# A fourth buffer for the words of the first 40 halves, in the tile of the slot sums and choices, and four halves fetched ahead

## The chip, the cores and the metric

The kernel runs on one core of one Trainium2 chip. The time is that of the device in microseconds (us); lower is better. A core has a matrix engine (TensorE, "PE"; "PEld" is its weight load), a vector engine (VectorE, "DVE"), an activation engine (ScalarE, "ACT"), a general engine (GpSimd, "POOL") and a fifth one (SyncE, "SP") that here does nothing but issue transfers. Each engine takes its own instructions strictly in the order in which they were written for it, and waits at an instruction whose inputs aren't there.

## What is computed

Three parts follow one another. Attention with a decay, over 4 x 8 heads of 576 tokens and 64 columns, gives `x` (2304 tokens by 512). A gated unit multiplies two products of `x`. A soft mixture of experts reduces 2304 tokens to 32 slots, runs 8 experts on the slots and spreads the result over the tokens again.

```python
scores = scale * np.matmul(q, k.transpose(0, 1, 3, 2))
cum = np.cumsum(np.maximum(s, 0.0), axis=-1)
scores = np.where(causal, -1e9, scores + np.minimum(-(cum[..., :, None] - cum[..., None, :]), 0.0))
attn = softmax(scores);  x = np.matmul(attn, v)          # then (2304, 512)
...
a = x @ w1;  b = x @ w2
h = a * b @ w3;  x = h @ w_out                           # w1, w2, w3, w_out are float64
...
logits = x @ phi
d = softmax(logits, over tokens);  slot_input = d.T @ x  # 32 slots
slot_out[e] = np.maximum(slot_input[e] @ w1[e], 0.0) @ w2[e]
c = softmax(logits, over slots);  out = c @ slot_out
```

The four weights of the gated unit come as float64, and the kernel has to turn their 64-bit words into float32 by itself.

## The kernel before

**Words and halves.** The float64 weights lie in HBM as 64-bit integers ("words"). They come in tiles of 128 by 1024 words, and each tile in two halves of 128 by 512 words, 512 KB each. The list `TODO` gives the order: 8 tiles of `w12` (w1 and w2 together), 4 of `wot` and 8 of `w3t` (w_out and w3 turned), which are the first 40 halves, k = 0 to 39 (`N0` = 20 tiles); then 4 of `wo` and 8 of `w3`, which are loaded later in another way. For each half:

- `fetch_words(k)` issues one transfer on SP (L178) into a tile of the tag "words", of which there are `NRAW` = 3. A transfer into a buffer has to wait until the half that lay in it has been converted.
- `convert` makes float32 of it: one pass on ACT (L192), then three on DVE (L195, L196, L199), or for `wot` and `w3t` a second pass on ACT (L203) and two on DVE (L204, L207). In the rows the words are `raw_w`, `raw_wot` and `raw_w3t`.
- For `w12` the result is split in two parts, on ACT (L223) and POOL (L224), for the matrix products of the gated unit.
- `load(k)` does one step of this: it converts half k, and behind that it fetches half k + 3.

**Attention.** `att_fetch` loads q and k of one item (L287, L288, L290, into a tile also named `raw`), `att_prep` the rows of the decay (L312, L314), and `att_values` v (L298). The decay rows are worked out at the start and stored to HBM by `decay_store` (L166, L167, into `rows_d`); from the third item on they are read back from there. `att_scores` makes the scores (PE L349, DVE L352, ACT L357), `att_norm` scales them (L366, L367 on DVE, L370 on POOL), `att_transpose` turns them (PE L385, L399; ACT L387, L401), `att_pv` multiplies by v (`x_ps`, L110).

**Gated unit and slots.** `glu_half` is a group of 12 products (`gl`, L447). `slot_sums` adds into `z_acc` (128 by 512 floats), `slot_choice` writes `c_all` (128 by 20 by 32 floats).

**Order.** All steps of a stage are written as short functions and interleaved by their weights (`weave`). Three stages carry the first 40 halves: k = 0 to 7 beside the first attention items, k = 8 to 25 beside the second group of items and the first 16 groups of the gated unit, the rest beside the third group. A scheduler may then reorder the instructions of PE, DVE, ACT and POOL within what their data allow, by its own estimate of when each can run. SP alone keeps the order as written.

The four lines on which the change turns are these:

```python
raw = ap.tile([P, 512], I64, tag="words", name=f"raw_{kind}_{i}_{e}", bufs=NRAW)
nc.sync.dma_start(raw, ...)
...
if k + NRAW < 2 * N0:
    fetch_words(k + NRAW, ap)
```

Of the kernel before, what the change touches and what calls it, by code (L numbers as in the profile page):

```python
# [10 lines left out]
F32 = mybir.dt.float32  # L11
# [3 lines left out]
I64 = mybir.dt.int64  # L15
# [6 lines left out]
P = 128  # L22
# [6 lines left out]
NS = NE * SPE  # L29
# [18 lines left out]
def attn_glu_softmoe_kernel(  # L48
# [17 lines left out]
    cp = pool("const", 1)  # L66
# [17 lines left out]
    NW, NRAW, NG4, NX, NE_ = 8, 3, 4, 6, 11  # L84
# [34 lines left out]
    ident = cp.tile([P, P], F32, name="ident")  # L119
    v_sb = cp.tile([P, FC, NS], F32, name="v_sb")  # L120
    v_last = cp.tile([P, ND, 4, NS], F32, name="v_last")
    z_acc = cp.tile([P, 512], F32, name="z_acc")
    run_max = cp.tile([P, 2], F32, name="run_max")
    run_sum = cp.tile([P, 2], F32, name="run_sum")
    c_all = cp.tile([P, 20, NS], F32, name="c_all")

    rsum_t = [cp.tile([P, 5, 2], F32, name=f"rsum_{k}") for k in range(3)]
    for t in rsum_t:
# [41 lines left out]
    words = {}  # L170
    TODO = [("w12", i) for i in range(FC)] + [("wot", i) for i in range(4)] + [("w3t", i) for i in range(FC)]
    N0 = len(TODO)
    TODO += [("wo", i) for i in range(4)] + [("w3", i) for i in range(FC)]

    def fetch_words(k, ap):
        (kind, i), e = TODO[k // 2], k % 2
        raw = ap.tile([P, 512], I64, tag="words", name=f"raw_{kind}_{i}_{e}", bufs=NRAW)
        nc.sync.dma_start(raw, {"w12": w12, "wo": wo, "w3": w3, "wot": wot, "w3t": w3t}[kind][i, :, 512 * e : 512 * e + 512])  # L178
        words[k] = raw

# [94 lines left out]
    def att_fetch(n, ap):  # L275
        h, tiles = ITEMS[n]
        if h % 2 == 0:
            b, c = divmod(h // 2, H // 2)
            for blk, (_, nt, own) in enumerate(BLK):
                if own[0] in tiles:  # L280
                    x_t[b, blk, c] = xpl.tile([P, 2, nt], F32R, tag=f"x{blk}", name=f"x_{b}_{blk}_{c}", bufs=NX)
        q0, q1 = QT[tiles[0]][0], sum(QT[tiles[-1]])
        tag = ("raw", "qa", "qb")[n % 3] if n < NF32 else "raw"
        raw = ap.tile([P, 2, S], F32, tag=tag, name=f"raw_{n}", bufs=NRW)
        m = 64 if n < NF32 else P
        if q0:
            nc.sync.dma_start(raw[:m, 0, q0:q1], qk[h, 0, :m, q0:q1])  # L287
            nc.sync.dma_start(raw[:m, 1, :q1], qk[h, 1, :m, :q1])  # L288
        else:
            nc.sync.dma_start(raw[:m, :, :q1], qk[h, :, :m, :q1].rearrange("n p t -> p n t"))  # L290
        hd[n] = dict(raw=raw, q0=q0, q1=q1)
# [455 lines left out]
    with tc.tile_pool(name="att", bufs=1) as ap:  # L747
        phi_sb = ap.tile([P, KC, NS], F32, name="phi_sb")
        u_sb = ap.tile([P, FC, NS], F32, name="u_sb")
        decay_fetch()  # L750
        fetch_words(0, ap)
        att_fetch(0, ap)
        fetch_words(1, ap)
        att_fetch(1, ap)
        make_identity(nc, ident)
# [10 lines left out]
        for n in range(NDIR):  # L766
            att_prep(n, ap)
        att_fetch(2, ap)
        for k in range(2, NRAW):
            fetch_words(k, ap)  # L770
        decay_store()
        for n in range(NDIR, FAR):
# [14 lines left out]
        def load(k):  # L787
            i = k // 2 - 1
            if FC <= i < N0:
                (sum_rows if k % 2 else use_rows)(*TODO[i])  # L790
            if k < 2 * N0:
                load_words(k, ap)
            if k + NRAW < 2 * N0:
                fetch_words(k + NRAW, ap)

        def fetch_later(i):
            if i > N0:
                store_words(i - 1)
            if i < len(TODO):
                for e in range(2):  # L800
                    fetch_words(2 * i + e, ap)

        prep = [(1, lambda k=k: load(k)) for k in range(2 * N0 + 2)]
        more = []
        for i in range(N0, len(TODO)):
# [10 lines left out]
        k = GC - GB  # L816
# [12 lines left out]
    def big(where, name):  # L829
        if where == "w":  # L830
            return wp.tile([P, 2048], F32, tag="W", name=name, bufs=NW)
        if where == "t":
            return tp2.tile([P, 2048], F32, name=name)
        return ep.tile([P, 2048], F32, tag="E", name=name)
# [3 lines left out]
    for i in range(2):  # L838
        t = big("e", f"wo_t{i}").rearrange("p (i c) -> p i c", i=2)
# [3 lines left out]
    for i in range(4):  # L843
        t = big("e", f"w3_t{i}").rearrange("p (i c) -> p i c", i=2)
# [67 lines left out]
    for q in range(4):  # L912
        cols = slice(256 * q, 256 * q + 256)
        yps = psum(("acc", "sg")[q % 2], f"y_ps_{q}")
        for r in range(2):
            for j in range(4):
                f = 4 * r + j
# [10 lines left out]
    for r in range(2):  # L928
        for c in range(2):
            for j in range(4):  # L930
                f = 4 * r + j
# [199 lines left out]
```

## Time and profile before

| | us |
|---|---|
| median of 3 runs | 554.52 |
| the three runs | 548.87, 554.52, 554.88 |
| the profiled execution | 550.8 |
| its span, from first to last instruction | 549.0 |
| PE busy in it | 516.8 (94%) |
| DVE, ACT, POOL busy | 328.9, 310.7, 130.7 |

The profiled execution is one of its own, beside the three runs. 1.8 us of it lie outside the span. "Busy" of PE means that a product was under way, which isn't the same as PE at its peak: products overlap, and their ends are modelled.

### The profile page before, as it was taken

Reading aid. Unit: us, or ns where it says so; the run is one execution under the profiler, and the core shown is the slowest. Engines: PE = TensorE matmul, PEld = TensorE weight load, DVE = VectorE, ACT = ScalarE, POOL = GpSimd, SP = SyncE. Lnnn points to the kernel's source line nnn. Section 1 sums busy time; section 2 is a strip of 40 time slices with the busy share of each in tenths; the row PEclk is TensorE's granted clock in tenths of the full one; section 3 lists DMA queues with packets and bytes.
Section 4 is the critical chain, followed back from the end, with each engine's and each line's share of the span. In section 5 each row is a group of like instructions: output and inputs, shape, how many; then the busy total and the mean of one; then the engine's idle time right before and its main releaser. Section 6 shows DMA issues by size and latency. Waiting matters only on the chain.

```text
span 549.0 us, 11760 instructions
## 1 busy us (share of the span) xinstructions
PE 516.8 (94%) x4288; PEld 433.6 (79%) x4288; DVE 328.9 (60%) x1014; ACT 310.7 (57%) x845; POOL 130.7 (24%) x199
## 2 busy tenths in 40 slices
PE   2898899999899999999999999999999999989993
PEld 2577688787788898989979899899989899843452
DVE  7568797879886484866667668467631211252433
ACT  4576676778785574766677567558644211321222
POOL 5475663103553241111211311111310000000000
PEclk9999999999899999999999999999999999999998
DMA  5856965877673263563557437453504999689977
GB/s 145 251 160 192 282 219 194 282 242 254 206 230 112 88 170 109 164 204 127 170 171 221 165 104 225 155 172 125 162 39 152 414 412 365 245 293 424 421 294 240
DMA packets 38809, 118.03 MB, mean 215 GB/s; under 512 B 4224, under 2 KB 10560, under 8 KB 35296
## 3 DMA queue, kind: packets, MB, share of 16 engines
q1 hardware_dynamic: 36768, 113.60, 61.0%
q10 hardware_dynamic: 1984, 3.69, 2.4%
q8 instruction: 34, 0.56, 0.4%
q14 instruction: 23, 0.19, 0.1%
HBM read 102.11 MB, written 11.60 MB: 207 GB/s over the span
## 4 chain that ended last, share of the span: by engine, by line
PE 70%; DMA 12%; DVE 9%; issue 3%; ACT 2%; POOL 1%; SPq 1%; DVEq 0%; ACTq 0%; POOLq 0%
PE gl L447 31%; PE x_ps L110 7%; PE sc_ps L349 7%; DMA raw_w<-in_w 5%; PE pt_ps L385 5%; PE gn_ps L617 3%; PE o_ps L1032 3%; PE h_ps L994 3%; DMA raw_w3t<-in_w3t 3%; PE ptd_ps L399 2%; PE z_ps L110 2%; DMA raw<-in_qk 2%; DVE sc L352 1%; PE lg L110 1%; POOL sc L370 1%
## 5 line engine op out<-in xcount | busy, mean ns | idle before, releaser
L447 PE MATMUL gl<-x,w12t 128*128 128x320 f32 (+1 forms) x1536 | 236.2, 303 | 1.0 <-DVE gC L465 1.0
L447 PEld LDWEIGHTS gl<-x,w12t 128*128 128x128 f32 x1536 | 211.2, 189 | 8.9 <-issue 4.2
L370 POOL TENSOR_SCALAR sc<-sc,rinv 128x64 f32<-128x64 f32 (+4 forms) x160 | 100.8, 648 | 254.1 <-DVE rinv L367 77.4
L357 ACT ACTIVATE sc<-sc,nmax 128x64 f32<-128x64 f32 (+4 forms) x160 | 89.9, 564 | 30.7 <-DVE nmax L352 28.2
L352 DVE CUSTOM_DVE_ANT_0 sc<-sc_ps,mask 128x64 f32<-128x64 f32 (+4 forms) x160 | 65.0, 422 | 32.4 <-PE sc_ps L349 31.5
L387 ACT COPY pt<-pt_ps 128x128 f32<-128x128 f32 (+3 forms) x128 | 52.8, 425 | 34.9 <-PE pt_ps L385 26.0
L385 PE MATMUL pt_ps<-ident,sc 128*128 128x128 f32 x320 | 56.9, 287 | 4.7 <-POOL sc L370 2.3
L385 PEld LDWEIGHTS pt_ps<-ident,sc 128*128 128x128 f32 x320 | 38.6, 145 | 16.5 <-issue 7.1
L453 ACT COPY a<-gl 128x256 f32<-128x256 f32 (+1 forms) x64 | 25.4, 399 | 45.5 <-PE gl L447 40.3
L349 PE MATMUL sc_ps<-qa 128*128 128x64 f32 (+1 forms) x144 | 46.8, 337 | 2.0 <-DVE gT L465 0.8
L110 PE MATMUL x_ps<-pt,v 128*64 128x256 f32 (+1 forms) x384 | 47.4, 358 | 0.0
L349 PE MATMUL sc_ps<-raw 68*128 68x288 f32 (+4 forms) x96 | 35.3, 513 | 11.1 <-DMA raw<-rows 9.6
L349 PE MATMUL sc_ps<-qb 68*128 68x64 f32 (+1 forms) x144 | 43.9, 307 | 0.1
L110 PEld LDWEIGHTS x_ps<-pt,v 128*64 128x64 f32 x384 | 33.5, 140 | 5.8 <-issue 1.0
L349 PEld LDWEIGHTS sc_ps<-raw 68*128 68x128 f32 x96 | 21.1, 260 | 16.1 <-issue 12.2
L192 ACT ACTIVATE w_w<-raw_w 128x512 f32<-128x512 f32 x32 | 21.5, 673 | 18.4 <-DMA raw_w<-in_w 18.3
L435 DVE TENSOR_TENSOR x<-x_ps,x 128x320 fp32r<-128x320 f32 (+1 forms) x32 | 14.1, 452 | 29.1 <-ACT x L434 29.1
L620 ACT COPY gn<-gn_ps 128x512 f32<-128x512 f32 x40 | 22.6, 586 | 15.5 <-PE gn_ps L617 14.9
L349 PEld LDWEIGHTS sc_ps<-qa 128*128 128x128 f32 x144 | 27.7, 193 | 4.3 <-DVE gT L465 1.3
L357 ACT ACTIVATION_READ_ACCUMULATOR sc<-sc,nmax 128x1 f32 x160 | 31.0, 194 | 0.0
L349 PEld LDWEIGHTS sc_ps<-qb 68*128 68x128 f32 x144 | 27.7, 192 | 0.9 <-issue 0.5
L399 PE MATMUL ptd_ps<-ident,sc 128*128 128x128 f32 x160 | 26.4, 291 | 2.1 <-ACT pt L387 1.9
(180 smaller groups left out, 726.5 us busy)
## 6 DMA issues: line engine op xcount, KB each, us to landing
ew<-in_ew SPq DMA_DIRECT2D x27, 1024.0 KB
raw_w<-in_w SPq DMA_DIRECT2D x32, 512.0 KB
raw<-in_qk SPq DMA_DIRECT2D x24, 576.0 KB
v<-in_v SPq DMA_DIRECT2D x16, 576.0 KB
raw_w3t<-in_w3t SPq DMA_DIRECT2D x16, 512.0 KB
raw_wot<-in_wot SPq DMA_DIRECT2D x8, 512.0 KB
raw_wo<-in_wo SPq DMA_DIRECT2D x8, 512.0 KB
w_d<-w_w SPq DMA_DIRECT2D x8, 512.0 KB
```

The costliest lines, as they stand in the source:

```text
L110: mm = nc.tensor.matmul(out_, lhs, rhs, start=start, stop=stop)
L192: line_up(nc.scalar.activation(out=w, in_=hi.bitcast(F32), func=AF.Copy, scale=F64_SCALE))
L349: nc.tensor.matmul(pp[:r, : z - a], x[:, 0, q0 : q0 + r], x[:, 1, a:z], start=x is mul[0], stop=x is mul[-1])
L352: nc.vector.tensor_tensor_reduce(out=sc[:r, a:z], in0=pp[:r, : z - a], in1=hd["mask"][:r, m0 : m0 + z - a], scale=-0.125, scalar=3.0e38 if ...
L357: nc.scalar.activation(out=sc[:r, :W], in_=sc[:r, :W], func=AF.Exp, bias=nmax[:r, i : i + 1], scale=-1.0, accum_out=rsum[:r, i, 0:1],)
L370: nc.gpsimd.tensor_scalar(out=sc, in0=sc, scalar1=rinv[:, i : i + 1], scalar2=1.0, op0=ALU.mult, op1=ALU.mult)
L385: nc.tensor.transpose(tp[:, j * P : (j + 1) * P], sc[:, j * P : (j + 1) * P], ident)
L387: t["turned", i] = nc.scalar.copy(out=pt[:, p0 : p0 + step * (i - 1) + 1 : step], in_=tp[:, : i * P].rearrange("p (j q) -> p j q", q=P))
L399: nc.tensor.transpose(dg[:, p0 : p0 + P], t["sc"][:, c0 : c0 + P], ident)
L447: nc.tensor.matmul(acc[:, :nt], w12_t[fc][:, wi, n, kc], x_t[b, blk, kc][:, xi], start=k == 0, stop=k == 3 * KC - 1)
L453: st["a_copy"] = nc.scalar.copy(out=a_sb[:, :nt], in_=acc[:, :nt])
L620: st["turned", blk, k, h] = nc.scalar.copy(out=gn[:r, 4 * h : 4 * h + 4].rearrange("p c f -> p (c f)"), in_=tp[:r])
```

## The change

The tiles `z_acc` and `c_all` become two parts of one tile, `spare_words`, of the same total size (4608 bytes in each partition). Nothing is written to either of them until the first 40 halves have been converted, in the order of the program. Up to then 4096 bytes of it serve as a fourth buffer: of the first 40 halves, every fourth (k = 3, 7, ... 39) goes there, the other three of four go to the tiles of the tag "words". Before the loop four halves are fetched instead of three, and `load(k)` fetches half k + 4 instead of k + 3. Only the first 40 halves are concerned. Line numbers behind the change are higher by one to four: L178 becomes L182, L192 becomes L196, L357 becomes L361, L166 becomes L167, and so on.

```diff
-    z_acc = cp.tile([P, 512], F32, name="z_acc")
+    spare_words = cp.tile([P, 256 + 10 * NS], I64, name="spare_words")
+    z_acc = spare_words.bitcast(F32)[:, :512]
...
-    c_all = cp.tile([P, 20, NS], F32, name="c_all")
+    c_all = spare_words.bitcast(F32)[:, 512:].rearrange("p (t s) -> p t s", s=NS)
...
     def fetch_words(k, ap):
         (kind, i), e = TODO[k // 2], k % 2
-        raw = ap.tile([P, 512], I64, tag="words", name=f"raw_{kind}_{i}_{e}", bufs=NRAW)
+        if k < 2 * N0 and k % (NRAW + 1) == NRAW:
+            raw = spare_words[:, :512]
+        else:
+            raw = ap.tile([P, 512], I64, tag="words", name=f"raw_{kind}_{i}_{e}", bufs=NRAW)
...
         att_fetch(2, ap)
-        for k in range(2, NRAW):
+        for k in range(2, NRAW + 1):
             fetch_words(k, ap)
         decay_store()
...
-            if k + NRAW < 2 * N0:
-                fetch_words(k + NRAW, ap)
+            if k + NRAW + 1 < 2 * N0:
+                fetch_words(k + NRAW + 1, ap)
```

On SP, at the start of the program, this stood in a row before (`raw_w_1_0` is half 2, `raw_w_1_1` half 3; `rows_d` are the decay rows, `raw_156`, `raw_163` and `raw_180` are q and k of the third to fifth attention item):

```order
L290 DMA raw_156<-in_qk 64x2x320
L178 DMA raw_w_1_0_158<-in_w 128x512
L166 DMA rows_d<-rows_130 32x4x512
L166 DMA rows_d<-rows_131 32x4x512
L167 DMA rows_d<-rows_132 256x1x64
L290 DMA raw_163<-in_qk 64x2x320
L314 DMA raw_156<-rows_d 4x2x320
L298 DMA v_176<-in_v 128x640
L314 DMA raw_163<-rows_d 4x2x320
L290 DMA raw_180<-in_qk 64x2x320
L178 DMA raw_w_1_1_209<-in_w 128x512
```

And now (`spare_words` is half 3, `raw_w_2_0` half 4):

```order
L294 DMA raw_155<-in_qk 64x2x320
L182 DMA raw_w_1_0_157<-in_w 128x512
L182 DMA spare_words<-in_w 128x512
L167 DMA rows_d<-rows_129 32x4x512
L167 DMA rows_d<-rows_130 32x4x512
L168 DMA rows_d<-rows_131 256x1x64
L294 DMA raw_163<-in_qk 64x2x320
L318 DMA raw_155<-rows_d 4x2x320
L302 DMA v_176<-in_v 128x640
L318 DMA raw_163<-rows_d 4x2x320
L294 DMA raw_180<-in_qk 64x2x320
L182 DMA raw_w_2_0_209<-in_w 128x512
```

The fetch of half 3 moved up past the stores of the decay rows, and half 4 stands where half 3 stood. So it goes on: at each later place of a fetch on SP the next half is fetched.

On ACT, a little later at the start, the conversion of half 3 stood behind the first softmax passes (L357) of the third item before:

```order
L192 ACTIVATE w_w_1_0_317<-raw_w_1_0_158 128x512
L357 ACTIVATE sc_167,rsum_94<-sc_167,nmax_186 128x192
L357 ACTIVATE sc_167,rsum_94<-sc_167,nmax_186 128x320
L387 COPY pt_218<-pt_ps_1_220 128x128
L387 COPY pt_218<-pt_ps_2_223 128x2x128
L223 CAST w12t_316<-w_w_1_0_317 128x512
L401 COPY ptd_219<-ptd_ps_227 128x192
L357 ACTIVATE sc_233,rsum_95<-sc_233,nmax_232 128x64
L357 ACTIVATE sc_233,rsum_95<-sc_233,nmax_232 128x192
L192 ACTIVATE w_w_1_1_381<-raw_w_1_1_209 128x512
```

And now:

```order
L196 ACTIVATE w_w_1_0_317<-raw_w_1_0_157 128x512
L361 ACTIVATE sc_167,rsum_93<-sc_167,nmax_186 128x192
L196 ACTIVATE w_w_1_1_381<-spare_words 128x512
L361 ACTIVATE sc_167,rsum_93<-sc_167,nmax_186 128x320
L391 COPY pt_218<-pt_ps_1_220 128x128
L391 COPY pt_218<-pt_ps_2_223 128x2x128
L227 CAST w12t_316<-w_w_1_0_317 128x512
L405 COPY ptd_219<-ptd_ps_227 128x192
```

The conversion of half 3 moved up by seven places, ahead of a softmax pass of the second item. Elsewhere on ACT, DVE, POOL and PE instructions changed places by up to 39 rows; the last sixth of the list of PE and the last twelfth of those of ACT and DVE stand as they stood.

## Rows read from the trace of the kernel before

**Rows 1.** Busy time by stretch: us, busy us of each engine, clock, DMA share, GB/s.
```profile
14.00:41.00 27.00, 23.97 (x89) 17.64 (x90) 15.39 (x65) 18.12 (x62) 14.99 (x25) 1.00 0.68 204
41.00:82.00 41.00, 37.02 (x253) 29.71 (x250) 35.13 (x78) 28.67 (x72) 23.93 (x21) 1.00 0.77 232
55.00:69.00 14.00, 11.77 (x83) 9.26 (x82) 10.97 (x23) 8.73 (x22) 8.58 (x8) 1.00 0.96 284
82.00:123.00 41.00, 39.58 (x304) 32.27 (x302) 32.67 (x84) 30.05 (x72) 6.50 (x8) 1.00 0.71 240
123.00:165.00 42.00, 39.17 (x361) 33.45 (x360) 37.91 (x116) 34.36 (x99) 19.58 (x24) 0.96 0.69 226
206.00:274.00 68.00, 68.00 (x579) 63.03 (x579) 42.91 (x133) 42.43 (x117) 13.18 (x25) 1.00 0.50 156
274.00:412.00 138.00, 137.21 (x1173) 125.79 (x1172) 88.79 (x281) 89.56 (x251) 28.84 (x51) 1.00 0.49 153
```

**Rows 2.** Chain that ended last, pieces that are transfers: start us, us, what.
```profile
11.61 4.83 DMA rows_d<-rows
...
23.27 4.93 DMA raw_w<-in_w
...
44.47 4.82 DMA raw_w<-in_w
...
54.64 7.27 DMA raw_w<-in_w
...
109.50 5.68 DMA raw_w3t<-in_w3t
...
122.42 4.33 DMA raw_w3t<-in_w3t
...
153.40 4.56 DMA raw_w3t<-in_w3t
```

**Rows 3.** Timeline of ACT, conversions behind these transfers; in brackets the idle before.
```profile
28.28 0.67 ACT L192 ACTIVATE w_w<-raw_w 128x512 f32<-128x512 f32 x1 [0.89 <-DMA raw_w<-in_w]
...
49.37 0.66 ACT L192 ACTIVATE w_w<-raw_w 128x512 f32<-128x512 f32 x1 [0.89 <-DMA raw_w<-in_w]
...
61.99 0.67 ACT L192 ACTIVATE w_w<-raw_w 128x512 f32<-128x512 f32 x1 [0.63 <-DMA raw_w<-in_w]
...
115.21 0.68 ACT L192 ACTIVATE w3t<-raw_w3t 128x512 f32<-128x512 f32 x1 [0.95 <-DMA raw_w3t<-in_w3t]
...
126.77 0.67 ACT L192 ACTIVATE w3t<-raw_w3t 128x512 f32<-128x512 f32 x1 [1.15 <-DMA raw_w3t<-in_w3t]
...
157.98 0.71 ACT L192 ACTIVATE w3t<-raw_w3t 128x512 f32<-128x512 f32 x1 [1.21 <-DMA raw_w3t<-in_w3t]
```

**Rows 4.** Waits of ACT from 14 to 165 us: total us, times, longest.
```profile
ACT w_w L192 <- DMA raw_w<-in_w: 9.6, 8, 2.2
ACT w3t L192 <- DMA raw_w3t<-in_w3t: 7.5, 8, 1.4
...
ACT wot L192 <- DMA raw_wot<-in_wot: 2.4, 2, 2.2
```

**Rows 5.** Timeline of ACT, conversion of half 2.
```profile
15.14 0.67 ACT L192 ACTIVATE w_w<-raw_w 128x512 f32<-128x512 f32 x1 [1.47 <-DMA raw_w<-in_w]
```

**Rows 6.** Timeline of SP: start us, us, what it issues.
```profile
10.45 0.59 SPq L178 DMA_DIRECT2D raw_w<-in_w  x1
11.15 0.84 SPq L166 DMA_DIRECT2D rows_d<-rows  x2
...
19.14 0.59 SPq L178 DMA_DIRECT2D raw_w<-in_w  x1
...
53.51 0.52 SPq L178 DMA_DIRECT2D raw_w<-in_w  x1
```

**Rows 7.** Waits of SP's queue from 14 to 165 us: total us, times, longest.
```profile
SPq L178 <- DVE w3t L207: 38.4, 12, 5.6
...
SPq L178 <- DVE wot L207: 10.7, 5, 3.8
```

**Rows 8.** Instructions on `raw_w3t`, and on `c_all`: duration ns, first and last start us.
```profile
L178 SPq DMA_DIRECT2D raw_w3t<-in_w3t x16: 327/328/329, 101.3 to 156.5; - x16
...
L207 DVE SCALAR_TENSOR_TENSOR w3t<-raw_w3t,w3t x16: 651/678/1059, 109.4 to 168.3; 128x512 int32<-128x512 int32 x16
...
L542 DVE TENSOR_TENSOR c_all<-ct_ps,mx x12: 177/216/226, 195.2 to 485.3; 128x64 f32<-128x64 f32 x8, 64x32 f32<-64x32 f32 x4
```

## The prediction

> **What bounds the kernel now.** I read the busy time by stretch first. From 206 to 412 us PE is the bound and nothing else can be: it is busy 68.00 of 68 us and then 137.21 of 138, with DVE and ACT at under two thirds [rows 1]. All 40 halves have been converted by then: the last DVE pass on them starts at 168.3 us [rows 8]. So the change can't speed anything up behind some 170 us. What it can do is bring the point at which PE becomes full forward or push it back, and the rest, which is a fixed amount of PE work, moves with that point. The first 165 us are another regime. There PE does 89 products in the 27 us from 14 to 41 and 253 in the next 41, against 579 in 68 later [rows 1]: it is called busy most of the time, but it waits inside that. DVE is the fullest of the others, 35.13 of 41 us, 32.67 of 41 and 37.91 of 42 [rows 1].
>
> Then the chain of waits, to see what ends last in those 165 us. Transfers of words stand in it six times behind the first one [rows 2], so words do come late. How late is on the timeline of ACT, which is the first to touch a half: it stands idle before these six conversions for 0.89, 0.89, 0.63, 0.95, 1.15 and 1.21 us [rows 3], 5.7 us together. A transfer on the chain lasts 4 to 7 us, but only this last bit of it is time in which ACT had nothing else. Over the whole stretch from 14 to 165 us ACT waited 9.6 + 7.5 + 2.4 = 19.5 us for words [rows 4]; 1.47 of it were for half 2 [rows 5], whose fetch the change leaves where it is. 18.0 us are within reach of it.
>
> **The change part by part.** *Earlier fetches.* Each half from k = 3 on is fetched at the place where the half before it was fetched. For half 4 that is the place of 19.14 us instead of 23.27 [rows 2, 6], 4.1 us earlier; for the one fetched at 54.64 us it is the place of 53.51, 1.1 us earlier [rows 2, 6]. Against that stand lags of 0.63 to 1.21 us, so each of the six should be gone, the one at 61.99 us by the smallest margin, since it falls into the stretch where the DMA engines are 0.96 busy [rows 1, 3]. The gain is between 0 (ACT takes up the lag at once, but DVE is late next) and 18.0 us (every wait of ACT comes through to PE). I take the 5.7 us of the six waits on the chain, and count the other 12.3 at nothing, because DVE, busy 106 of the 124 us from 41 to 165 [rows 1], or the loads of v and of q and k come last there.
>
> *The start.* The fourth fetch stands ahead of the stores of the decay rows. On SP it takes 0.59 us to issue [rows 6]; that is the least that the stores come later. At the most they also come later by the 512 KB that go ahead: at the 284 GB/s of the fullest stretch [rows 1] that is 1.85 us, 2.4 together. The stores are on the chain: they took 4.83 us [rows 2], although their own 576 KB would take 2.1 at that rate; half 2 was issued just ahead of them at 10.45 us [rows 6], and 1.85 + 2.1 is most of the 4.83. That speaks for the upper end. Against it, from 14 to 41 us the DMA engines are only 0.68 busy [rows 1], so that the queue empties again and half 3 is missing from it later, at 19.14 us. I take the middle, 1.5 us.
>
> The Trainium skill has a rule on this ("DMA: Bandwidth & Descriptors", section "Queues, rings and completion order"): on each DMA engine descriptors of one queue are consumed in the order of its ring. By that rule the whole 512 KB stand ahead of the stores, and the loss would be 2.4 us and the net gain 3.3 instead of 4.2. The 4.83 us of the stores agree with it; no row shows what part of it reaches the end.
>
> *The order on the other engines.* The conversion of half 3 now stands ahead of a softmax pass of the second item on ACT. Half 2 was ready at 15.14 us [rows 5]; half 3 comes behind it by 1.85 us, at 17.0, so ACT waits there and then works 0.67 us. That delays copies which PE needs only for the first product with v, and the third item's scores wait for the decay rows anyway, so I put it at nothing while the stores are the later of the two; without that cover it costs some 1.5 us. The many small moves behind it I put at nothing too: where PE is full they can cost it no more than the 0.8 us by which it isn't full from 274 to 412 [rows 1]; before that they may go either way, and the range has to hold that.
>
> *What costs nothing.* The tile is no larger than the two it replaces. A fetch into the fourth buffer waits for the conversion of the half four back, at the place on SP where a fetch waited for the same conversion before: SP waits there as it did (38.4 and 10.7 us for `w3t` and `wot` [rows 7]), and v and the q and k behind it come neither sooner nor later for it, unless the conversions themselves come sooner. The first write of `c_all` is at 195.2 us, 27 us behind the last pass on the words [rows 8]; that distance covers the new dependence between them.
>
> Sum: 5.7 - 1.5 = 4.2 us off. The profiled execution of 550.8 us would become 546.6. It lies 3.7 below the median of the three runs; against that median, 554.5, the forecast is 550.3.
>
> **The rivals.** *The ring of buffers sets the pace.* The sixteen fetches of `w3t` are issued from 101.3 to 156.5 us [rows 8], one every 3.68 us, and twelve times SP waited for a conversion there [rows 7]. If the round trip (fetch, land, convert, fetch again) is what holds this stretch, three halves go through it in 11.0 us; four would do so in the same time, 2.76 us each, 13.8 us less over the 15 steps. DVE allows at most its idle time from 82 to 165 us, 83 - 70.6 = 12.4 [rows 1]. With the loss at the start that is 10.9 us off, 543.6. For it: the eight waits of ACT for `w3t` [rows 4]. Against it: each of them is at most 1.4 us of a period of 3.68, so most of the period is other work.
>
> *Something else is late by as much.* ACT's waits vanish, and DVE or the loads of v, q and k end at the same moment as before. Then only the start is left: 0 to 2.4 us more, near 555. For it: DVE is at 85% from 41 to 165 us. Against it: DVE itself is not full.
>
> *The words overtake attention.* At the start the stores lose 2.4 us and the early conversion 1.5 on ACT, and nothing is won: 3.9 us more, 558.4. This decides the sign as soon as the words' lag gives back less than 3.9 us, which is two thirds of what I count on. For it: attention, not the words, feeds PE at the start, and the stores were on the chain [rows 2]. Against it: the words fetched ahead are the same bytes, only sooner, and the queue has room.
>
> **How the numbers follow.** One per cent, about what a measurement of this kernel can tell from no change, is 5.5 us: 549.0 to 560.1. Chances: the forecast 0.42 (547 to 553); the pace of the ring 0.25 (539.5 to 547); something else late 0.17 (553 to 557); overtaken 0.16 (556 to 562). Faster by over 1%: all but a little of the second and a third of the first, 0.38. Slower by over 1%: the upper half of the last, 0.09. The rest, 0.53, is within 1%. The range of 541.5 to 557 leaves out the best third of the second case and most of the last, together about 0.2; it takes in both ends of the start's price.
>
> **What the profile after would show.** Waits of ACT for words from 14 to 165 us fall from 19.5 to a few us, and no transfer of words stands in the chain between 20 and 165 us. The last pass on `w3t` starts some 4 us sooner than 168.3, and everything behind it is shifted by that and otherwise alike. The stores of the decay rows land near 18 us instead of 16.4. Under the pace of the ring the fetches of `w3t` would come every 2.8 us; under the third case ACT's waits would have gone and the last pass still start near 168. I would be wrong if the words' lag were only the shadow of another wait, or if the order on PE, which moved in the whole first part, turned out better or worse by more than the words are worth.

## The result and the profile after

The changed kernel is slower: 559.94 us in the median of four runs (557.26 to 561.31) against 551.85 for the kernel before on the same chip (548.87 to 554.88, four runs). The ratio is 1.0138, interval 1.0096 to 1.018. The forecast was 550.3. The profiled execution took 560.15 us, its span 558.4. Medians and ratios in this document leave out the slow executions: one of 1703 us, one of 1255 us, and three of the kernel before between 554.8 and 557.4 us. In the lines of the changed kernel, L438 is the copy that takes the sums of v (L110) out of PSUM, before it was L434.

Busy time by stretch, columns as in [rows 1]:

```profile
14.00:41.00 27.00, 19.24 (x73) 13.71 (x73) 16.18 (x58) 16.10 (x51) 14.36 (x23) 1.00 0.66 187
41.00:82.00 41.00, 37.61 (x192) 28.25 (x192) 26.62 (x73) 25.63 (x67) 17.90 (x20) 0.75 0.69 204
82.00:123.00 41.00, 41.00 (x281) 32.71 (x281) 31.67 (x79) 29.56 (x69) 10.59 (x12) 1.00 0.67 223
...
274.00:412.00 138.00, 137.66 (x1196) 126.17 (x1198) 93.13 (x296) 91.98 (x254) 34.32 (x55) 1.00 0.51 160
```

Look at the counts beside PE and at the clock, not at the busy time. From 41 to 82 us PE is called busy for as long as before (37.61 against 37.02), but it does 192 products instead of 253, and the granted clock is 0.75 instead of 1.00 [rows 1]. DVE does 26.62 us of work there instead of 35.13. By the table further down the seventh fetch of v goes out 12.8 us late, the twelfth 9.4, and the span ends 9.4 us late (558.4 against 549.0). So the loss was made in the first 85 us, where the forecast expected three of the six waits to go.

The pieces of the chain of waits that are transfers of words, start and us:

```profile
11.05 6.13 DMA spare_words<-in_w
...
25.39 6.03 DMA raw_w<-in_w
...
117.95 7.13 DMA spare_words<-in_w3t
...
128.25 5.44 DMA spare_words<-in_w3t
134.72 6.39 DMA raw_w3t<-in_w3t
...
155.91 4.42 DMA spare_words<-in_w3t
```

Words are fetched earlier, and still they stand in the chain [rows 2]. The waits of ACT from 14 to 165 us say how that can be:

```profile
ACT w_w L196 <- DMA raw_w<-in_w: 8.2, 5, 2.1
...
ACT wot L196 <- DMA raw_wot<-in_wot: 4.3, 5, 1.3
...
ACT spare_words L207 <- DMA spare_words<-in_w3t: 2.9, 1, 2.9
...
ACT w_w L196 <- DMA spare_words<-in_w: 2.6, 2, 2.1
```

With the smaller rows of this view (1.8, 1.6, 0.8 and 0.3) they sum to 22.5 us, against 19.5 before [rows 4]. The conversions have moved forward in ACT's order along with the fetches, and wait as they did. A new wait is on SP, same stretch:

```profile
SPq L302 <- PE x_ps L110: 54.8, 8, 10.6
SPq L182 <- DVE w3t L211: 21.7, 11, 3.2
```

and in the kernel before:

```profile
SPq L298 <- PE x_ps L110: 19.4, 5, 6.8
```

SP's queue now stands 54.8 us for the sums of v (it may not load a v before PE is done with an older one), and everything that is written behind it, q, k, decay rows and words, stands with it. When these fetches of v are issued is a good clock for the whole first part. The times are those of SP's timeline; the runs in the lower rows come further down:

| kernel | 1st fetch of v | 3rd | 4th | 5th | 7th | 9th | 12th |
|---|---|---|---|---|---|---|---|
| before | 17.26 | 32.73 | 42.49 | 51.53 | 71.58 | 104.36 | 171.47 |
| after | 19.37 | 36.64 | 50.24 | 60.70 | 84.41 | 116.53 | 180.86 |
| after, order of before | 20.43 | 35.70 | 44.02 | 52.32 | 70.85 | 103.57 | 168.86 |
| before and idle load, order of before | 20.07 | 36.39 | 46.07 | 56.16 | 76.30 | 109.54 | 176.76 |
| own order from 41 us on | 20.13 | 35.66 | 49.59 | 64.11 | 84.18 | 120.09 | 183.84 |
| own order up to 41 us | 20.39 | 38.78 | 48.29 | 56.60 | 75.60 | 108.31 | 171.69 |

After is 2.1 us late at the first, 3.9 at the third, 7.8 at the fourth and 12.8 at the seventh.

### The profile page after: what moved, and what is told of

It reads as the page before. It is cut to its first block, busy times and chain, and to the rows that moved or that the text cites. A ratio compares the mean times of both kernels' runs of the same rounds, so it can differ in the third digit from the quotient of the medians.

```text
span 558.4 us, 11762 instructions
## 1 busy us (share of the span) xinstructions
PE 522.2 (94%) x4288; PEld 435.9 (78%) x4288; DVE 326.1 (58%) x1014; ACT 313.1 (56%) x845; POOL 127.9 (23%) x199
## 4 chain that ended last, share of the span: by engine, by line
PE 75%; DMA 9%; ACT 8%; DVE 4%; issue 2%; SPq 1%; ACTq 0%; DVEq 0%
PE gl L451 32%; PE sc_ps L353 9%; PE x_ps L110 8%; PE pt_ps L389 6%; PE gn_ps L621 3%; DMA spare_words<-in_w3t 3%; PE o_ps L1036 3%; PE h_ps L998 3%; PE ptd_ps L403 3%; ACT sc L361 2%; PE z_ps L110 2%; DMA raw_w<-in_w 2%; DMA raw_wo<-in_wo 1%; PE lg L110 1%; DMA raw_w3t<-in_w3t 1%
## 5 line engine op out<-in xcount | busy, mean ns | idle before, releaser
L451 PE MATMUL gl<-x,w12t 128*128 128x320 f32 (+1 forms) x1536 | 240.3, 306 | 2.2 <-DVE gC L469 1.5
L451 PEld LDWEIGHTS gl<-x,w12t 128*128 128x128 f32 x1536 | 214.7, 192 | 10.3 <-issue 4.6
L374 POOL TENSOR_SCALAR sc<-sc,rinv 128x64 f32<-128x64 f32 (+4 forms) x160 | 97.4, 627 | 257.1 <-DVE rinv L371 108.0
L361 ACT ACTIVATE sc<-sc,nmax 128x64 f32<-128x64 f32 (+4 forms) x160 | 89.9, 563 | 29.0 <-DVE nmax L356 27.7
L356 DVE CUSTOM_DVE_ANT_0 sc<-sc_ps,mask 128x64 f32<-128x64 f32 (+4 forms) x160 | 65.5, 423 | 38.4 <-PE sc_ps L353 34.9
L353 PE MATMUL sc_ps<-raw 68*128 68x288 f32 (+4 forms) x96 | 37.8, 537 | 12.9 <-DMA raw<-rows 9.6
L110 PE MATMUL x_ps<-pt,v 128*64 128x256 f32 (+1 forms) x384 | 47.8, 361 | 0.0
L110 PEld LDWEIGHTS x_ps<-pt,v 128*64 128x64 f32 x384 | 32.6, 142 | 7.5 <-issue 2.6
L361 ACT ACTIVATION_READ_ACCUMULATOR sc<-sc,nmax 128x1 f32 x160 | 30.8, 192 | 0.0
L469 DVE TENSOR_TENSOR gU<-gl,a 128x256 f32<-128x256 f32 (+1 forms) x20 | 8.7, 435 | 34.4 <-PE gl L451 28.1
L228 POOL TENSOR_TENSOR w12t<-w_w,w12t 128x512 fp32r<-128x512 f32 x16 | 23.2, 1456 | 20.8 <-ACT w12t L227 20.7
```

Source lines behind the costliest of these rows:

```text
L110: mm = nc.tensor.matmul(out_, lhs, rhs, start=start, stop=stop)
L228: nc.gpsimd.tensor_tensor(out=tl, in0=w, in1=th.bitcast(F32), op=ALU.subtract)
L353: nc.tensor.matmul(pp[:r, : z - a], x[:, 0, q0 : q0 + r], x[:, 1, a:z], start=x is mul[0], stop=x is mul[-1])
L356: nc.vector.tensor_tensor_reduce(out=sc[:r, a:z], in0=pp[:r, : z - a], in1=hd["mask"][:r, m0 : m0 + z - a], scale=-0.125, scalar=3.0e38 if ...
L361: nc.scalar.activation(out=sc[:r, :W], in_=sc[:r, :W], func=AF.Exp, bias=nmax[:r, i : i + 1], scale=-1.0, accum_out=rsum[:r, i, 0:1],)
L374: nc.gpsimd.tensor_scalar(out=sc, in0=sc, scalar1=rinv[:, i : i + 1], scalar2=1.0, op0=ALU.mult, op1=ALU.mult)
```

## The experiments

Each kernel was timed in five rounds beside the kernel before on the same chip. Medians of before were 551.2, 550.5, 549.8, 551.5 and 549.0 us for the five groups below, so runs of different groups are compared by their ratios to it.

### Undoing single parts, order left free

**Half 3's first fetch back at its old place**, four halves ahead from then on.

```diff
-        for k in range(2, NRAW + 1):
+        for k in range(2, NRAW):
...
+            if k == 0:
+                fetch_words(NRAW, ap)
```

> The changed kernel with one thing undone: the first fetch of half 3 goes back to its place before (behind the decay rows, with half 4 right behind it); the fourth buffer and four halves ahead stay from there on. Before 551.9, after 559.9. Theory 1 (512 KB ahead of the decay rows starve PE at the start, and the clock falls after it): decay rows are read back near 16.5 us instead of 18.6, full clock from 41 to 82 us, 547 to 553 us. Theory 2 (half 3's conversion ahead of a softmax pass on ACT): the same here, since the conversion goes back too. Theory 3 (what costs is fetching four ahead from then on, or the order that the scheduler makes of it): 557 to 561 us.

557.45 us, ratio 1.011 (1.0073 to 1.0147): theory 3. The read of the decay rows goes out at 16.32 us and the first fetch of v at 17.07, as before the change, and the loss stays.

**The kernel before and one idle load.** 512 KB that nobody reads, ahead of the stores of the decay rows; three buffers and all fetches as before.

```diff
+        nc.sync.dma_start(spare_words[:, :512], w12[1, :, 512:])
         decay_store()
```

(The tile `spare_words` is made as in the change.)

> The kernel before, three buffers and three halves ahead, with one more load of 512 KB ahead of the stores of the decay rows, into the tile of the slot sums and choices, that nothing reads. Theory 1: decay rows read back near 18.6 us, PE idle 2 us longer before 41 us, clock down between 41 and 82 us, 557 to 561 us. Theories 2 and 3: within 2 us of before, 550 to 554.

558.86 us, ratio 1.013 (1.0089 to 1.0171): theory 1, and the whole loss without a fourth buffer.

**Stores first.** The changed kernel with the stores ahead of halves 2 and 3.

```diff
+        decay_store()
         for k in range(2, NRAW + 1):
             fetch_words(k, ap)
-        decay_store()
```

> The changed kernel with the stores of the decay rows ahead of the fetches of halves 2 and 3. Theory 1: decay rows read back at 15 us or sooner, full clock to 82 us, 545 to 551 us. Theory 2: also below after, since halves 2 and 3 come late enough not to stand ahead of the second item, 550 to 554. Theory 3: 557 to 561.

557.77 us, ratio 1.0127 (1.01 to 1.0154): theory 3 again. The third fetch of v goes out at 30.73 us, 2.0 us ahead of the kernel before, and the fourth at 49.50, 7.0 us behind it. The loss is made between the two.

**Half 3's conversion later.** It is bound behind a softmax pass of the third item.

```diff
-            convert(k, w, False)
+            convert(k, w, False, hd[2]["exp", 1] if k == 3 else None)
...
-        nc.scalar.activation(
+        t["exp", i] = nc.scalar.activation(
```

> The changed kernel with the conversion of half 3 bound behind the softmax pass of the third item, as it stood before; its fetch stays early. Theory 1: nothing won, decay rows at 18.6 us, clock down from 41 to 82 us, 557 to 561. Theory 2: 550 to 554. Theory 3: 557 to 561.

557.62 us, ratio 1.0118 (1.0073 to 1.0164): theory 1 or 3.

No single part gives the loss back, not even the two edits that take the early transfer away from ahead of the stores; and yet a load that only takes up bandwidth makes all of it. No theory of the transfers alone fits both. But these four share something else: in each, the scheduler, which sets the order by a simulated timeline of its own, wrote another order for PE, ACT and DVE than before. Between before and after, 1976 of the 3440 products stand at another place of PE's list, though no product was touched. So order and transfers had to be taken apart.

### Holding the order, and filling the clock

**The changed kernel in the order of before.** At the end of the program all instructions of an engine are tied one behind the other; such an edge only sets a place. `ORDER` holds, for PE, ACT, DVE and POOL, the places that the instructions have in the list of the kernel before. SP's order is written by hand and stays that of the changed kernel.

```diff
+    none = mybir.DependencyInfo(mybir.DependencyClass.NoSync, mybir.DependencyReason.DATA)
+    for engine, places in ORDER.items():
+        own = [i for i in nc.cur_bb.bb.instructions if str(i.engine) == "EngineType." + engine]
+        for a, b in zip(places, places[1:]):
+            tc.add_manual_dep(own[b], own[a].name, none, reason="order")
```

> The changed kernel, its transfers untouched (fourth buffer, four halves ahead), but the instructions on PE, ACT, DVE and POOL are tied one behind the other into the order in which they stand in the kernel before. Theory of the order (the extra transfer at the start makes the scheduler write another order, in which PE waits more in the first 60 us): the loss goes, 549 to 553 us. Theory of the transfers (512 KB more at the start land ahead of what the attention waits for, whatever the order): it stays, 556 to 560 us. Theory of the clock: it follows whichever of the two leaves PE without gaps between 15 and 42 us; the products' durations fall to the short ones near 42 us if the time is near 551, near 60 us if it is near 559.

547.5 us, ratio 0.9946 (0.9924 to 0.9968): faster than both kernels. It is the version to keep. ACT's waits for words in it, from 14 to 165 us:

```profile
ACT w_w L196 <- DMA raw_w<-in_w: 3.5, 2, 2.0
...
ACT w3t L196 <- DMA spare_words<-in_w3t: 0.2, 1, 0.2
```

SP's wait for the sums of v in the same stretch:

```profile
SPq L302 <- PE x_ps L110: 17.6, 5, 6.1
```

Its busy time from 41 to 82 us, columns as in [rows 1]:

```profile
41.00:82.00 41.00, 39.02 (x267) 31.35 (x265) 36.69 (x83) 31.35 (x77) 25.27 (x23) 0.97 0.85 252
```

ACT waits 3.7 us for words instead of 19.5, no transfer of words stands in the chain between 20 and 165 us, PE does 267 products instead of 253. In these points it is what the prediction said the profile after would show.

**The kernel before in the order of after**, the same edges with the other list.

> The kernel before with its own three buffers and transfers, but with the instructions of PE, ACT, DVE and POOL tied into the order in which they stand in the changed kernel. Theory of the order: 556 to 560 us, with PE's durations long until some 60 us. Theory of the transfers: 549 to 553 us.

639.92 us, ratio 1.1617 (1.1577 to 1.1657), far beyond both expectations, which thought an order good or bad in itself. ACT's waits for words from 14 to 165 us:

```profile
ACT w_w L192 <- DMA raw_w<-in_w: 47.6, 6, 13.4
ACT wot L192 <- DMA raw_wot<-in_wot: 22.7, 2, 11.6
```

The order of after takes each half for granted earlier than three buffers can bring it, and ACT, which works its list in turn, stands 70 us. This run shows how tightly an order belongs to its transfers, but it can't tell what the order costs beside four buffers.

**Seven idle products on PE**, in the changed kernel and in the kernel before, each tied to its own order. In the profiles PE's products take the long durations of its lower level (1.2 GHz) until 42 us before and until 62 after (there but for 52 to 54 us), so half speed was a candidate for the cause.

```diff
         hd["ap"] = ap
+        warm_ps = psum("acc", "warm_ps")
+        for _ in range(7):
+            nc.tensor.matmul(warm_ps, ident, mask[:, :512], start=True, stop=True)
```

`ORDER` puts four of them ahead of the first scores and three into the idle stretches between 15 and 21 us.

> The changed kernel with its own order tied down on all four engines, and seven products of 512 columns that nobody reads on PE: four before the first scores, two and one in the two idle stretches between 15 and 21 us. Theory of the clock (the loss is PE at half speed until 62 us because it stood idle in between): PE's durations become short well before 40 us and the time falls to 545 to 553 us, though nothing is transferred or ordered otherwise. If the clock is a mere companion of a later start: 557 to 563 us.

561.9 us, ratio 1.0202 (1.0157 to 1.0247).

> The kernel before with its own order tied down and the same seven products on PE. Theory of the clock: it too runs at half speed for its first 42 us, so short durations come well before that, and the time falls below the kernel before: 540 to 549 us. If the clock is a mere companion: 550 to 554 us.

551.16 us, ratio 1.0022 (0.9995 to 1.005). Both times are those of a mere companion. But the test reaches less far than it looks. The idle products do raise the clock, for a while. PE in the kernel before with them, the scores of the first two items and a product of the first sums of v, 20 us later:

```profile
11.76 2.46 PE L349 MATMUL sc_ps<-raw 68*128 68x64 f32 x12
...
31.55 0.69 PE L110 MATMUL x_ps<-pt,v 128*64 128x256 f32 x1
```

The same, in the kernel before:

```profile
9.64 4.61 PE L349 MATMUL sc_ps<-raw 68*128 68x64 f32 x12 [9.64 <-DMA raw<-rows]
...
30.53 0.69 PE L110 MATMUL x_ps<-pt,v 128*64 128x256 f32 x1
```

The twelve score products take 2.46 us instead of 4.61, but they start 2.1 us later, behind the four idle products, and end at 14.22 us as they did (14.25). By the first sums the durations are long again, and the sums start no sooner. So speed in the first 30 us was bought with PE's own time, and nothing came of it. In the changed kernel with idle products, two blocks of wide scores behind 42 us read:

```profile
43.87 3.62 PE L353 MATMUL sc_ps<-raw 68*128 68x448 f32 x6
...
53.77 1.96 PE L353 MATMUL sc_ps<-raw 68*128 68x448 f32 x6 [0.68 <-issue]
```

From 53.77 us on PE is fast, some 8 us sooner than in after, and the time is no better; the run with the stores first has such a block of 1.96 us at 52.79, and loses 1.27%. Both speak against half speed from 54 to 62 us as what is lost. From 42 to 52 us PE is as slow here as in after, and no run takes that away and keeps the order of after. Whether the order costs its time through the clock there, this test can't tell.

### How much is the transfer, and where the order loses

**Half 3's first fetch late, order of before.** The first experiment's edit, and the edges.

> The changed kernel with half 3's first fetch back at its old place, behind the stores and among the attention's steps, and with the compute engines' instructions in the order of the kernel before. With the order held, the fourth fetch at the start cost some 3 us at 22 us (the fetches of v stood 3.2 us behind those of the kernel before in the kernel that differs by this fetch alone) and the fourth buffer gave some 6 us by 170 us. If these two terms are apart, this kernel keeps the second without the first: 543.5 to 546 us. If the fourth buffer's gain hangs on being four ahead from the start: 546.5 to 551 us.

548.26 us, ratio 0.9964 (0.9939 to 0.9989). The same as with the early fetch, not 2 to 4 us better: the second of the two expectations. Half 3 and half 4 are now fetched right ahead of the next decay rows. ACT waits for half 3, and PE, by the profile, for those rows:

```profile
23.93 0.66 ACT L196 ACTIVATE w_w<-spare_words 128x512 f32<-128x512 f32 x1 [2.80 <-DMA spare_words<-in_w]
...
26.60 2.47 PE L353 MATMUL sc_ps<-raw 68*128 68x64 f32 x6 [2.61 <-DMA raw<-rows_d]
```

**The kernel before and the idle load, order of before.**

> The kernel before with the idle load of 512 KB ahead of the decay rows' stores, as in the run that took 558.9 us, but with the compute engines' instructions in the order of the kernel before. Theory of the order (the load's loss was nearly all the new order): 550.5 to 554 us, of which the transfer itself is 0 to 3 us. Theory of the transfers: 556 to 560 us.

553.78 us, ratio 1.0067 (1.0038 to 1.0097). With the order free it was 1.013: about half of that loss was order. The other half, 0.67% or 3.7 us (2.1 to 5.3 by the interval), is the price of 512 KB ahead of the stores with nothing gained for it; the first fetch of v goes out 2.8 us later.

**The order of before up to the second pair's sums of v, its own from there**, and **the other way round**. The place is that of 39.53 us in the kernel before, behind 58 products. `ORDER` is spliced there, the transfers are those of after.

> The changed kernel with the compute engines in the order of the kernel before up to the second pair's sums of v (58 products of PE and what stands ahead of them on the others, to some 41 us), and in the changed kernel's own order from there. If the cost of the order lies behind that place (the wide scores set ahead of the sums of v, at half clock), 555 to 560 us; if ahead of it (transposes and scores of the first items in another order), 547 to 551 us.

560.0 us, ratio 1.0185 (1.0146 to 1.0224).

> The counterpart: the changed kernel's own order up to the same place, the order of the kernel before from there. If the cost of the order lies ahead of the place, 555 to 560 us; if behind it, 547 to 551 us. With the run that has the two the other way round, the two losses should add up to some 12 us.

550.11 us, ratio 0.9978 (0.9945 to 1.0011). The loss lies behind that place: there the changed kernel's own order costs 2.4% against the order of before throughout (0.9946). What stands ahead of it, the early conversion of half 3 among it, costs 0.3%, which the intervals don't tell from nothing. Together that is some 15 us, where 12 were expected and after itself loses 10.5; the intervals don't tell whether the two halves really add up to more than the whole.

At that place the two lists read so on PE (item 8's wide scores, the second pair's sums of v, and the next transposes). Before:

```
L399 MATMUL ptd_ps_3_376<-ident_86,sc_2_233 128x128 x3
L110 MATMUL x_ps_2_0_390<-ptd_2_327,v_3_248 64x64
L385 MATMUL pt_ps_4_1_428<-ident_86,sc_4_341 128x128
L110 MATMUL x_ps_2_0_390<-ptd_3_368,v_3_248 64x64
...
L385 MATMUL pt_ps_4_2_441<-ident_86,sc_4_341 128x128 x2
L349 MATMUL sc_ps_8_3_0_562<-raw_8_360 128x448
L349 MATMUL sc_ps_8_4_0_572<-raw_8_360 128x288
L349 MATMUL sc_ps_8_4_1_575<-raw_8_360 128x288
```

After:

```
L403 MATMUL ptd_ps_3_376<-ident_86,sc_2_233 128x128 x3
L353 MATMUL sc_ps_8_3_0_561<-raw_8_360 128x448
L353 MATMUL sc_ps_8_4_0_571<-raw_8_360 128x288
L353 MATMUL sc_ps_8_4_1_574<-raw_8_360 128x288
L110 MATMUL x_ps_2_0_389<-ptd_2_327,v_3_248 64x64
```

The three wide products have moved ahead of the sums. And on ACT, in the kernel before, the copies of item 4's transposes and of the sums come first, in after they come behind the conversion of half 8, two rounding copies for halves 7 and 8 and two wide softmaxes. ACT's timeline of before:

```profile
42.49 0.42 ACT L434 CAST x<-x_ps 128x320 fp32r<-128x320 f32 x1 [0.24 <-PE x_ps L110]
43.61 0.68 ACT L192 ACTIVATE w_w<-raw_w 128x512 f32<-128x512 f32 x1 [0.38 <-DMA raw_w<-in_w]
44.34 0.67 ACT L357 ACTIVATE sc<-sc,nmax 128x448 f32<-128x448 f32 x1
```

and of after:

```profile
45.67 0.67 ACT L196 ACTIVATE w_w<-raw_w 128x512 f32<-128x512 f32 x1 [0.73 <-DMA raw_w<-in_w]
46.25 0.60 ACT L227 CAST w12t<-w_w 128x512 fp32r<-128x512 f32 x1
46.76 0.67 ACT L361 ACTIVATE sc<-sc,nmax 128x448 f32<-128x448 f32 x1
...
48.56 0.78 ACT L361 ACTIVATE sc<-sc,nmax 128x576 f32<-128x576 f32 x1 [1.04 <-DVE nmax L356]
...
49.80 0.62 ACT L227 CAST w12t<-w_w 128x512 fp32r<-128x512 f32 x1 [0.37 <-DVE w_w L203]
50.32 0.26 ACT L391 COPY pt<-pt_ps 128x128 f32<-128x128 f32 x1
50.48 0.43 ACT L438 CAST x<-x_ps 128x320 fp32r<-128x320 f32 x1
```

The copy of the sums starts at 50.48 us instead of 42.49. But it is not ACT that holds the fourth fetch of v, which goes out at 50.24, ahead of this copy. That fetch waits for PE's sums. Their last products, and the wide ones, in the kernel before:

```profile
41.69 0.77 PE L110 MATMUL x_ps<-ptd,v 128*64 128x64 f32 x8
...
42.66 1.89 PE L349 MATMUL sc_ps<-raw 68*128 68x448 f32 x6
```

and in after:

```profile
43.53 3.75 PE L353 MATMUL sc_ps<-raw 68*128 68x448 f32 x6
...
49.37 0.84 PE L110 MATMUL x_ps<-ptd,v 128*64 128x64 f32 x8
```

The sums end at 50.21 us instead of 42.46, and the wide products ahead of them take 3.75 us, about the step from 3.9 to 7.8 us in the table of v. They take double the 1.89 us of the kernel before, because PE is at its lower level there: by these durations about half of the step is the place and half the clock.

### Which engine, and is one place enough

**The stretch from the second pair's sums to the fifth's in the order of after, all else in that of before**: for all four engines (some 41 to 63 us), for PE alone, and for ACT, DVE and POOL alone.

> The changed kernel in the order of the kernel before, but between the second pair's sums of v and the fifth's (120 products of PE, 43 instructions of ACT, 43 of DVE, 15 of POOL; some 41 to 63 us) in its own order. If the loss is made in this stretch, 555 to 560 us; if in what its own order does later, 547 to 551 us.

556.04 us, ratio 1.0097 (1.0062 to 1.0131).

> The same stretch, PE alone in the changed kernel's order (two moves: the three wide score products of item 8 ahead of the second pair's sums of v, and five transposes of item 4 ahead of the wide scores), ACT, DVE and POOL in that of the kernel before. If the late sums of v are the cost, 553 to 560 us; if the cost is on ACT, 547 to 551 us.

555.0 us, ratio 1.0058 (1.0032 to 1.0084).

> The same stretch, ACT, DVE and POOL in the changed kernel's order (on ACT the conversions of two halves, three rounding copies and two wide softmaxes ahead of the copies of item 4's transposes and of the second pair's sums), PE in that of the kernel before. If the queue on ACT is the cost, 553 to 560 us; if the late sums on PE are, 547 to 551 us.

556.44 us, ratio 1.0083 (1.0054 to 1.0113). Against 0.9946 with the order of before throughout, the stretch costs 1.5%, PE's two moves alone 1.1%, the moves on the other three alone 1.4%. So neither engine alone is the place, and the two don't add up. The fifth fetch of v, at 52.32 us with the order of before, goes out at 60.74 with PE's moves, at 60.97 with the others' and at 62.52 with both: either set makes nearly the whole delay. With PE's moves ACT waits for the sums, from 41 to 62 us (0.9 us with the order of before):

```profile
ACT pt L391 <- PE x_ps L110: 8.9, 2, 4.5
```

PE itself waits no longer in this stretch than with the order of before (1.1 us against 1.5), but it keeps to the long durations until some 61 us, not 43. Its wide products with PE's moves:

```profile
42.06 3.75 PE L353 MATMUL sc_ps<-raw 68*128 68x448 f32 x6
...
52.56 3.62 PE L353 MATMUL sc_ps<-raw 68*128 68x448 f32 x6
```

and with the order of before throughout:

```profile
44.20 1.89 PE L353 MATMUL sc_ps<-raw 68*128 68x448 f32 x6
...
47.25 1.96 PE L353 MATMUL sc_ps<-raw 68*128 68x448 f32 x6 [0.72 <-DVE w_w L199]
```

In this run the delay stands in products of double length, not in waits of PE.

With the moves of the others PE waits for ACT's copy of the transposes, 7.5 us, and goes over to the long durations behind it. The wide products ahead of that wait and the next ones behind it:

```profile
42.02 1.89 PE L353 MATMUL sc_ps<-raw 68*128 68x448 f32 x6
51.42 0.90 PE L403 MATMUL ptd_ps<-ident,sc 128*128 128x128 f32 x3 [7.51 <-ACT pt L391]
...
52.35 3.75 PE L353 MATMUL sc_ps<-raw 68*128 68x448 f32 x6
```

**One edge.** The changed kernel, free order, with the first wide product of item 8 set behind the second pair's sums.

```diff
+        return mm
...
-                nc.tensor.matmul(pp[:r, : z - a], x[:, 0, q0 : q0 + r], x[:, 1, a:z], start=x is mul[0], stop=x is mul[-1])
+                mm = nc.tensor.matmul(pp[:r, : z - a], x[:, 0, q0 : q0 + r], x[:, 1, a:z], start=x is mul[0], stop=x is mul[-1])
+                if n == 8 and i == 3:
+                    tc.add_manual_dep(mm.ins, st["pv", 2].ins.name, mybir.DependencyInfo(mybir.DependencyClass.NoSync, mybir.DependencyReason.DATA), reason="order")
...
+        st["pv", n] = group(products, [hd[n + e]["turned", i] for e in range(2) for i in (tiles[-1], "d")])
```

> The changed kernel, free order, with one edge added: the first wide score product of item 8 stands behind the last product of the second pair's sums of v on PE. The scheduler then sets the copies of the transposes and of the sums on ACT ahead of the wide softmaxes again. If the loss is this one place, 547 to 552 us; if it is many small places of the new order, 554 to 560 us.

564.31 us, ratio 1.0221 (1.0186 to 1.0257). Slower than after itself. The copies on ACT did move back ahead of the softmaxes, and the scheduler, given one place, wrote yet another order elsewhere; SP waits 54.5 us for the sums of v as in after, and the fourth fetch goes out at 49.73 us, as late as there. One displaced group is not the whole of it; but since the rest of the order moved too, this run doesn't price that place alone.

**Controls.** The kernel before tied to its own order, and the changed kernel with the stores first, in the order of before.

> The kernel before, nothing changed but that its compute engines' instructions are tied, by edges that only set a place and wait for nothing, into the order in which they stand anyway. If such edges cost nothing, 549 to 552 us, within 0.3% of the kernel before; if the tied runs owe their time to the edges, it moves like them.

548.61 us, ratio 1.0004 (0.9979 to 1.003): the edges have no time of their own.

> The changed kernel with the decay rows' stores ahead of the fetches of halves 2 and 3, in the order of the kernel before on the compute engines. If the 512 KB ahead of the stores are what the fourth fetch costs at the start (3 us at 20 us in the run that differs by nothing else), the rows come back before 17 us and the time is 543.5 to 546.5 us, faster than all others; if the words are wanted as early as the rows (half 2's conversion then waits), 546.5 to 550 us.

546.98 us, ratio 0.9957 (0.993 to 0.9985): the same as with the stores behind, and the second of the two expectations. The read of the decay rows goes out at 15.06 us, but now the words of half 2 are late. ACT stands 4.73 us for them, and its copy of the transposes, which stands behind, lets PE's next weight load go:

```profile
18.77 0.66 ACT L196 ACTIVATE w_w<-raw_w 128x512 f32<-128x512 f32 x1 [4.73 <-DMA raw_w<-in_w]
...
20.89 0.52 ACT L391 COPY pt<-pt_ps 128x128 f32<-128x128 f32 x2
...
21.19 0.50 PEld L403 LDWEIGHTS ptd_ps<-ident,sc 128*128 128x128 f32 x3 [5.41 <-ACT pt L391]
```

(The profile puts the wait of the matmuls themselves, 5.00 us, down to a load of v; but they read `sc` and `ident` alone.)

## Why the prediction was wrong

**The step that failed: "the many small moves behind it I put at nothing too".** The prediction looked at the order of SP and ACT at the start and had a bound for PE, 0.8 us, only where PE is full. Ahead of that it allowed "either way" but gave no price and no rival, and too little room: the range ended at 557. It did name the order on PE, at its end, among what would prove it wrong. The measured price of the new order, the changed kernel against itself in the order of before, is 1.0138 / 0.9946 = 1.019, some 10.5 us of 551. As far as the intervals tell, all of it lies behind the second pair's sums of v; the 22 us from there to the fifth pair's make 1.5%. What PE and ACT then do is read above: wide products stand ahead of awaited sums, at double length, and conversions and wide softmaxes ahead of awaited copies.

**The words' lag: right in kind, and with the order held near in size.** Forecast was a net gain of 4.2 us of 550.8, or 0.76%. With the order held it is 0.54% (0.32 to 0.76), 3.0 us. ACT's waits went from 19.5 to 3.7 us, and the last pass on the words starts at 166.1 us instead of 168.3 (4 us sooner was forecast). In the changed kernel itself nothing of it is seen, because the scheduler moved the conversions forward with the fetches: 22.5 us of waits, and a last pass at 174.0.

**The start: too small.** The fourth fetch was priced at 1.5 us with 0.59 and 2.4 as bounds. The read of the decay rows goes out 2.1 us later in after (18.61 instead of 16.50 us), and the first fetch of v 2.1 to 3.2 us later in the runs with it. The 512 KB by themselves, order held and nothing gained by them, cost 3.7 us (2.1 to 5.3 by the interval): more than the 1.5, while the upper bound lies within the interval. By the difference of that run to the one with the fourth buffer, 1.0067 against 0.9946, the buffer would give 6.7 us, near the forecast 5.7. But the two are not apart: with the fetch late or the stores first the total is the same (0.9964, 0.9957), and the wait only goes over to other rows or to the words. So the net stands, and its division stays open. The rule of the Trainium skill ("DMA: Bandwidth & Descriptors", "Queues, rings and completion order") that descriptors of one queue are taken in the order of the ring agrees with the delay of 2.1 us, near the 2.4 worked out with it; no run here tells it from a mere sharing of bandwidth.

**The waits of SP that were said to stay.** 38.4 and 10.7 us became 35.7 and 10.4 with the order held: right. In after 21.7 us are left of the first, because SP already stood at the fetches of v.

**The rival "the words overtake attention"** named 558.4 us and slower, near what came, but by another mechanism: with all transfers of the change in place and the order held the kernel is faster than before, and the moves ahead of 41 us, half 3's conversion among them, came to 0.3%.

**Open.** What the order loses behind 63 us: with its own order from 41 us to the end the kernel takes 1.0185, with the stretch alone 1.0097. Which of its moves that are was not taken apart. How much of the price is paid through the clock is open too. In after PE waits only 1.2 us from 41 to 62 us, and its loss there stands in long durations; with PE's moves alone it is the same; with the others' moves PE first waits 7.5 us, and the long durations come behind. The order makes each of these, since the transfers are the same, but no run held PE fast from 42 to 52 us in the order of after. Nor was the changed kernel tied to its own order without idle products; only for the kernel before is it shown that the edges cost nothing.

## What to carry to other kernels

Where a scheduler sets the order, a change of transfers is also a change of order on every engine: here the transfers were worth 0.5% and the order that came with them 1.9%. Price it in the forecast, with both signs, by looking at which late group moved ahead of which awaited one on PE and ACT in the first stage that isn't bound by one engine; and before an edit is dropped, run it with the old order tied down, which cost nothing by itself here (1.0004); a list made for other transfers can cost a lot (1.1617). Undoing parts of an edit under a free scheduler tells little, since each undoing makes a new order: of four such runs here the idle load pointed at the start and two others away from it, while the loss was made behind 41 us.

## What was not expected of the hardware

The column of the granted clock reads 1.00 from 20 to 40 us in the kernel before, where a product of 128x256 with v took 0.69 us (at 30.53 us), as it did at 0.50 in after; in the order-held run it took 0.43 us at 51.08. Nor does this end at 40 us: with PE's moves alone the column reads 1.00 from 41 to 62 us, where the wide products took 3.75 and 3.62 us. In this kernel the durations of one form, not that column, tell the level.
